# Attention and MoE on one core: q, k and v loads per head, spread over the DMA queue, with new ranks

## Chip, core and metric

The kernel runs on one core of a Trainium2 chip: TensorE (PE) with its weight loads (PEld), VectorE (DVE), ScalarE (ACT), GpSimd (POOL) and the SP queue, which issues nearly all DMAs. The metric is device time in microseconds, the median of several runs. Before the change it is 813.95 us (three runs, 813.47 to 814.06).

## What is computed

```python
q_pool = q.reshape(B, H, S // 2, 2, D).mean(axis=3)          # B 4, H 8, S 1152, D 64
scores = (1 / sqrt(D)) * matmul(q_pool, k.T)                 # 576 x 1152 for each head
attn = softmax(scores)                                       # row maximum, exp, division by the sum
x = matmul(attn, v), heads side by side                      # 2304 tokens x 512
h = x @ w_in                                                 # 512 x 2048
g = h * sigmoid(1.702 * h)
out = g @ w_out                                              # 2048 x 512
```

## The kernel before

Heads are worked in 16 pairs of two. Pairs 0 to 3 are "wide": their products run in fp32, and TensorE turns q, k and the exponentials. Pairs 4 to 15 split every operand into two fp16 halves (`hi` and `lo`), and the DMA engines turn q, k and p by `dma_start_transpose` on the SP queue. Each pair has nine score tiles, numbered n (0 to 143). One tile of pairs 4 to 15 passes through: `scores` S on TensorE; `row_max` M on VectorE, which also frees the PSUM buffer of the scores (there is one); `lift` B, an addition of a constant to the maximum, on VectorE or GpSimd; `exps` E on ScalarE; `p_hi` H, the fp16 cast, on ScalarE or VectorE; `p_lo` L, the subtraction of that cast, on VectorE or GpSimd; `p_tr` T, the transpose of both halves on SP; and, once four tiles of both heads are there (the ninth tile alone), `pv` on TensorE. There are three buffers of p, of hl (the two fp16 halves) and of pt (the transposed).

Before a pair's first score tile comes its preparation: `q_load`, `k_load` and `v_load` from memory (two heads each; q has one DMA of 256 KB and one of 32 KB per head, k and v one of 288 KB), `q_add` on GpSimd, maxima of q, k and v on VectorE (`q_max`, `kv_max`), a scale of all three (`rows_max`, `max_all`, `qkv_scale`), the fp16 halves (`q_hi`, `q_lo`, `k_hi`, `k_lo`, `v_hi`, `v_lo`) and the transposes `q_tr` and `k_tr`. The scale needs all three maxima, so `q_tr` stands behind the last of the three loads. There is one buffer of q and of k as loaded, and two of v.

The MoE weights are loaded in 32 pieces, scaled and split (`w_hi`, `w_lo`) while attention runs. The MoE itself works on nine blocks of 256 tokens, eight steps each: `moe_h` (24 matmuls), `moe_tanh`, `moe_gate`, `moe_hi`, `moe_lo` and `moe_o` (12 matmuls). 24 h and 12 o matmuls are called a unit here; there are 72. Their ranks are above those of all attention work, so TensorE takes them where attention has nothing ready, and the rest stands behind attention.

What stands where on each engine is decided while the program is built. `Plan.order` plays all tasks through with a cost for each and, engine by engine, takes of the tasks that can start soon (within `wait`) the one of lowest rank; the tasks are then written out in that order. Each engine works its instructions strictly in this order. `rank` is the table of ranks and offsets, `movable` lists the tasks that may also run on a second engine. DMAs are played as one line: each takes its `dma` on it and lands `DMA_OUT` later. `gate` holds the loads of a pair back, in that play, until tile n0 - 10 (n0 is the pair's first tile).

Of the kernel before, what the change touches and what calls it, by code (L numbers as in the profile page):

```python
# [23 lines left out]
class Plan:  # L24
# [10 lines left out]
    DMA_IN, DMA_OUT, SWITCH = 0.3, 2.0, 0.095  # L35
# [4 lines left out]
    def add(self, name, eng, cost, rank, fn, after=(), take=(), use=(), dma=0.0, or_on=None, two=False, mode=0):  # L40
        t = dict(name=name, rank=rank, fn=fn, take=list(take), dma=dma, two=two, mode=mode)
# [19 lines left out]
    def order(self):  # L61
# [30 lines left out]
        while len(out) < len(self.tasks):  # L92
# [30 lines left out]
            for h in heirs.get(t["name"], ()):  # L123
                for e in h["on"]:
                    at = free[e] if e == eng and (e == "PE" or h["name"][0] == t["name"][0] == "T") else seen
                    ready[id(h), e] = max(ready[id(h), e], at)
# [9 lines left out]
def kernel(  # L136
# [40 lines left out]
    ACT_LOADS = 99  # L177
# [5 lines left out]
        w1=672.363352, w1_rate=1.175392, w2=1244.868308, w2_rate=0.001398, w1_cut=1489.334692,  # L183
        w1_cut_rate=0.001424, w2_cut=-595.061438, w2_cut_rate=0.001, v_max=2164.84965, load=-651.503117,
        prep=119.711174, max=-168.143312, exp=275.487608, p_hi=-1337.520533, p_lo=698.818424, pv=859.763092,
        x=177.140321, recip=-285.189077, w_tr=458.776726, w_ev=564.091585, g=-2167.171137, pv_b=-936.761133,
        max_b=829.453772, p_lo_b=1852.826129, prep_b=-1240.661907, v=2173.398754, lift=363.803036,
# [52 lines left out]
    def dve(n, psum=False, fast=False):  # L240
        return n / (1920 if fast else 960) + (0.065 if psum else 0.068)
# [152 lines left out]
    def queue(g):  # L394
        return nc.scalar if g.P >= ACT_LOADS else nc.sync

    def k_load(g):
        t = new("kraw", ("kraw", g.P), [128, 2, KR, D], F32)
        for a in range(2):
            (queue(g) if g.P else nc.scalar).dma_start(out=t[:, a], in_=k[g.b, 2 * g.pr + a].rearrange("(p r) d -> p r d", r=KR))  # L400

    def q_load(g):
        t = new("qraw", ("qraw", g.P), [128, NJ, 2, D], F32)
        for a in range(2):
            full, last = q[g.b, 2 * g.pr + a, 0:1024], q[g.b, 2 * g.pr + a, 1024:S]
            queue(g).dma_start(
                out=t[:, 4 * a:4 * a + 4].rearrange("p (u t) r d -> p u (t r d)", u=2),
                in_=full.rearrange("(u p t r) d -> p u (t r d)", u=2, t=2, r=2),
            )
            queue(g).dma_start(  # L410
                out=t[64 * a:64 * (a + 1), NJ - 1].rearrange("p r d -> p (r d)"),
                in_=last.rearrange("(i r) d -> i (r d)", r=2),
            )
# [114 lines left out]
    def v_load(g):  # L528
        t = new("vraw", ("vraw", g.P), [128, 2, KR, D], F32)
        for a in range(2):  # L530
            queue(g).dma_start(out=t[:, a], in_=v[g.b, 2 * g.pr + a].rearrange("(p r) d -> p r d", r=KR))
# [17 lines left out]
    def maxima(g, r):  # L549
        G, f, qa = g.P, first_max(g), ("qkva", g.P)  # L550
        plan.add(("v_max", G), "DVE", dve(1152), r, lambda g=g: kv_max(g, "v"),
                 [("v_load", G)] + ([] if g.wide else [("q_max", G)]), use=[("vraw", G)])
# [5 lines left out]
    for g in pairs:  # L558
# [7 lines left out]
        vr = ("vraw", G)  # L566
        on_act, ahead = G >= ACT_LOADS, n0 + rank["load"]
        le, slow = ("ACT", 0.0) if on_act else ("SP", 0.3)
# [561 lines left out]
```

## Time and profile before

| what | value |
|---|---|
| median of 3 runs | 813.95 us |
| profiled execution: its own time | 812.64 us |
| profiled execution: span | 810.6 us |
| PE busy | 769.4 us, 95% of the span |
| DVE busy | 627.6 us, 77% |
| ACT busy | 538.9 us, 66% |
| POOL busy | 329.2 us, 41% |
| packets of the SP queue (q1) | 127.10 MB, 76.4% of 16 DMA engines' span |

The span runs from the first to the last instruction of the profiled execution; 2.0 us more lie around it. Busy shares are of the whole span. Pairs 0 to 3 take the first 160 us, pairs 4 to 15 the time to about 690 us, and the last 120 us are MoE alone, with ACT and DVE lightly used and the DMA queue nearly empty. So the share of a whole span hides what is full in the middle, and the views below are read by stretch. A busy matmul is not one at full rate, since ends of matmuls are modelled.

### The profile page before, as it was taken

Reading aid. Unit: us, or ns where it says so; the run is one execution under the profiler, and the core shown is the slowest. Engines: PE = TensorE matmul, PEld = TensorE weight load, DVE = VectorE, ACT = ScalarE, POOL = GpSimd, SP = SyncE. Lnnn points to the kernel's source line nnn. Section 1 sums busy time; section 2 is a strip of 40 time slices with the busy share of each in tenths; the row PEclk is TensorE's granted clock in tenths of the full one; section 3 lists DMA queues with packets and bytes.
Section 4 is the critical chain, followed back from the end, with each engine's and each line's share of the span. In section 5 each row is a group of like instructions: output and inputs, shape, how many; then the busy total and the mean of one; then the engine's idle time right before and its main releaser. Section 6 shows DMA issues by size and latency. Waiting matters only on the chain.

```text
span 810.6 us, 16793 instructions
## 1 busy us (share of the span) xinstructions
PE 769.4 (95%) x6756; PEld 514.7 (64%) x6756; DVE 627.6 (77%) x1019; ACT 538.9 (66%) x782; POOL 329.2 (41%) x274
## 2 busy tenths in 40 slices
PE   6999999998999889999999999989898999999997
PEld 3556655656566557666767667756566676666664
DVE  4776998799999998888989789789989885322222
ACT  4888888888686867777667767776677674322222
POOL 3155533366366446454534445363445544000000
PEclk9999999999999999999999999999999999999999
DMA  8255533578999999999999999999999998000001
GB/s 295 74 202 161 163 109 130 160 154 152 210 198 207 174 210 165 184 232 205 205 189 218 213 191 190 218 200 203 174 215 183 173 157 155 2 27 1 27 1 27
DMA packets 336142, 128.77 MB, mean 159 GB/s; under 512 B 311232, under 2 KB 321472, under 8 KB 336064
## 3 DMA queue, kind: packets, MB, share of 16 engines
q1 hardware_dynamic: 335776, 127.10, 76.4%
q8 instruction: 53, 0.87, 0.4%
q10 hardware_dynamic: 288, 0.59, 0.2%
q14 instruction: 25, 0.20, 0.1%
HBM read 45.09 MB, written 4.72 MB: 61 GB/s over the span
## 4 chain that ended last, share of the span: by engine, by line
PE 54%; DVE 24%; DMA 7%; issue 7%; ACT 6%; POOL 1%; SPq 1%; DVEq 0%; ACTq 0%; POOLq 0%
PE h L951 14%; PE o L987 12%; DVE p L668 7%; PE s L654 6%; PE pv L733 5%; PE s L625 5%; DMA pt<-hl 4%; PE o L745 4%; PE pv L768 4%; DVE g L976 2%; ACT hl L248 2%; DVE wbuf L322 2%; DVE gf L965 2%; DVE hl L707 2%; PE h L304 1%
## 5 line engine op out<-in xcount | busy, mean ns | idle before, releaser
L668 DVE TENSOR_SCALAR_CACHE_REDUCE p<-s,e_s 128x1152 f32<-128x1152 f32 x144 | 203.0, 1410 | 26.6 <-PE s L625 10.9
L707 POOL TENSOR_TENSOR hl<-p,hl 128x1152 f16<-128x1152 f32 x77 | 191.9, 2493 | 62.0 <-ACT hl L248 46.1
L675 ACT ACTIVATE p<-p,nm 128x1152 f32<-128x1152 f32 x144 | 179.8, 1249 | 48.7 <-DVE nm L697 31.1
L987 PE MATMUL o<-wbuf,g 128*128 128x512 f16 x864 | 206.2, 380 | 0.0
L951 PEld LDWEIGHTS <-wbuf 128*128 128x128 f16 x1728 | 167.8, 98 | 41.9 <-issue 6.9
L248 ACT ACTIVATE hl<-p 128x1152 f16<-128x1152 f32 x105 | 121.4, 1158 | 26.4 <-DMA pt<-hl 22.5
L654 PE MATMUL s<-kT,qT 128*128 128x384 f16 (+1 forms) x720 | 123.5, 327 | 13.9 <-DVE p L668 12.5
L987 PEld LDWEIGHTS <-g 128*128 128x128 f16 x864 | 82.8, 98 | 84.5 <-issue 3.0
L951 PE MATMUL h<-x16a,wbuf 128*128 128x256 f16 x960 | 116.4, 273 | 3.1 <-DVE gf L965 3.1
L959 ACT ACTIVATE th<-h,t_s 128x512 f32<-128x512 f32 x72 | 49.3, 684 | 95.7 <-PE h L951 94.6
L965 DVE SCALAR_TENSOR_TENSOR gf<-th,h 128x512 f32<-128x512 f32 x72 | 49.2, 683 | 77.2 <-ACT th L959 77.1
L654 PEld LDWEIGHTS <-qT 128*128 128x128 f16 (+1 forms) x720 | 61.9, 100 | 59.8 <-issue 25.3
L951 PE MATMUL h<-wbuf 128*128 128x256 f16 x768 | 92.8, 275 | 0.0
L733 PEld LDWEIGHTS <-vhl 128*64 128x64 f16 x1944 | 80.8, 111 | 15.8 <-issue 14.5
L976 DVE SCALAR_TENSOR_TENSOR g<-gf,g 128x512 f16<-128x512 f32 x72 | 62.9, 873 | 17.0 <-ACT g L248 16.7
L733 PE MATMUL pv<-pt,vhl 128*64 128x256 f16 x1296 | 75.7, 273 | 0.0
L248 ACT ACTIVATE g<-gf 128x512 f16<-128x512 f32 x51 | 32.0, 627 | 37.8 <-DVE gf L965 37.7
L686 POOL TENSOR_SCALAR w_r<-w_d 128x4 f32<-128x4 f32 (+1 forms) x48 | 17.6, 366 | 96.5 <-ACT p L675 94.0
L745 PE MATMUL o<-idf,p 128*128 128x128 f32 x324 | 50.2, 283 | 2.3 <-ACT pt L248 2.3
L248 ACT ACTIVATE pt<-o 128x384 f32<-128x384 f32 x96 | 43.4, 484 | 13.0 <-PE o L745 11.3
L625 PE MATMUL s<-kT,qT 64*128 64x512 f32 (+3 forms) x240 | 49.4, 523 | 1.4 <-DVE p L668 1.3
L299 POOL TENSOR_TENSOR wbuf<-raw 128x512 f32<-128x512 f32 x32 | 34.7, 1091 | 37.8 <-ACT raw L295 37.8
(103 smaller groups left out, 857.9 us busy)
## 6 DMA issues: line engine op xcount, KB each, us to landing
vraw<-in_v_dram SPq DMA_DIRECT2D x32, 288.0 KB, 5.2
kraw<-in_k_dram SPq DMA_DIRECT2D x30, 288.0 KB, 4.5
qraw<-in_q_dram SPq DMA_DIRECT2D x32, 256.0 KB, 3.4
raw<-in_moe_w_in_dram SPq DMA_DIRECT2D x16, 512.0 KB, 5.2
raw<-in_moe_w_out_dram SPq DMA_DIRECT2D x16, 512.0 KB, 4.3
out_dram<-osb SPq DMA_DIRECT2D x16, 256.0 KB, 3.4
pt<-hl SPq DMA_TRANSPOSE x96, 5.0
qraw<-in_q_dram SPq DMA_DIRECT2D x32, 32.0 KB, 3.0
```

The costliest lines, as they stand in the source:

```text
L248: nc.scalar.activation(out=out, in_=in_, func=ACTF.Copy, scale=1.0 if scale is None else scale)
L625: nc.tensor.matmul(out=ps[m, bank, 0:128 * (last - first)], lhsT=qT[h, (j - half) % NJ, m], rhs=kT[h, first:last].rearrange("p j c -> p (j ...
L654: nc.tensor.matmul(out=ps[m, c, 0:384], lhsT=st, rhs=T["kT", g.P][:, o:o + 3].rearrange("p r c -> p (r c)"), start=(l == 0), stop=(l == 1),)
L668: nc.vector.tensor_scalar(out=p, in0=s, scalar1=e_s[:, g.P:g.P + 1], scalar2=None, op0=ALU.mult, op1=ALU.min, accum_out=m)
L675: nc.scalar.activation(out=p, in_=p, func=ACTF.Exp, bias=T["nm", n], scale=-1.0, accum_out=sm)
L707: (nc.vector if e == "DVE" else nc.gpsimd).tensor_tensor(out=t[:, 1, :], in0=T["p", n].rearrange("p c f -> p (c f)"), in1=t[:, 0, :], op=A ...
L733: nc.tensor.matmul(out=ps[64 * a:64 * (a + 1), 0:w], lhsT=T["vhl", g.P][:, a, g.block[a][c], m], rhs=pt[:, l * KR + c, o:o + w], start=(pa ...
L745: nc.tensor.transpose(ps[:, 128 * i:128 * (i + 1)], T["p", n][:, c, 128 * i:128 * (i + 1)], idf)
L951: nc.tensor.matmul(out=h[:, e, :], lhsT=w1(2 * j + e, l, kk), rhs=x_rhs(blk, m, kk), start=(kk == 0 and l == 0 and m == 0), stop=(kk == KD ...
L965: nc.vector.scalar_tensor_tensor(out=gf, in0=T["th", blk, j], scalar=1.0, in1=T["h", blk, j].rearrange("p e n -> p (e n)"), op0=ALU.add, o ...
L976: nc.vector.scalar_tensor_tensor(out=g[:, 1].rearrange("p e n -> p (e n)"), in0=T["gf", blk, j], scalar=2.0 ** -16, in1=g[:, 0].rearrange( ...
L987: nc.tensor.matmul(out=o, lhsT=g[:, l, e, 128 * t:128 * (t + 1)], rhs=w2(fc, m), start=(fc == 0 and l == 0 and m == 0), stop=(fc == KFF - ...
```

## The change

Four things.

The loads. `q_load`, `k_load` and `v_load` now load one head (`a`) each and are six tasks. They may be played from tile n0 - 14 on, one tile apart (q, q, k, k, v, v), so that they come to stand between the transposes. They are the same DMAs as before.

The planner's picture of the DMA queue. A transpose (`tr`) now occupies the SP queue until it is through: at least 2.9 us, and 1.84 us after the DMA before it; it lands 2.05 us later. A load takes 1.05 us per head instead of 2.0 or 2.3 for two; it enters after 0.8 us and lands 1.6 us after its end.

The ranks. All of `rank`, `wait` and `movable` are new. `lift` may no longer run on POOL; `k_hi` and `q_hi` may now run on DVE, `v_hi` may not.

The unused loads from the ACT queue (`ACT_LOADS`) are gone. Nothing is computed in another way.

```diff
-    DMA_IN, DMA_OUT, SWITCH = 0.3, 2.0, 0.095
+    DMA_IN, DMA_OUT, SWITCH = 0.8, 1.6, 0.095
...
-            if t["dma"]:
+            if t["tr"]:
+                free[eng] = dma_free = max(end, dma_free + t["dma"])
+                end = dma_free + 2.05
+            elif t["dma"]:
                 dma_free = max(s + self.DMA_IN, dma_free) + t["dma"]
                 end = dma_free + self.DMA_OUT
...
     rank = dict(
-        w1=672.363352, w1_rate=1.175392, w2=1244.868308, w2_rate=0.001398, w1_cut=1489.334692,
+        w1=1971.8069114113, w1_rate=22.2436521906, w2=2562.6136217615, w2_rate=0.1126475672,
...
-    movable = dict(DVE=('x', 'x_hi', 'w_hi', 'p_hi', 'v_hi', 'moe_hi', 'w_spread', 'qk_ev', 'w_sign'), POOL=('p_lo', 'w_exp', 'lift'))
-    wait = dict(PE=0.021, ACT=0.488, DVE=0.092, POOL=0.65)
+    movable = dict(DVE=('x_hi', 'p_hi', 'x', 'w_hi', 'k_hi', 'moe_hi', 'q_hi', 'qk_ev'), POOL=('p_lo', 'w_exp'))
+    wait = dict(PE=0.005839, ACT=0.318681, DVE=0.098398, POOL=1.168057)
...
-        plan.add(("q_load", G), le, 2.1, ahead, lambda g=g: q_load(g), gate, take=[("qraw", qr)], dma=1.8 + slow)
-        plan.add(("k_load", G), le if G else "ACT", 1.0, ahead + 0.1, lambda g=g: k_load(g), gate, take=[("kraw", kr)],
-                 dma=2.0 + slow)
...
-        plan.add(("v_load", G), le, 1.0, v_at, lambda g=g: v_load(g), v_gate, take=[("vraw", vr)], dma=2.0 + slow)
+        for i, (what, a) in enumerate((w, a) for w in "qkv" for a in range(2)):
+            key = (what + "raw", G)
+            at, after, eng = n0 + rank["load"] + 0.1 * i, [("E", n0 - 14 + i)] if n0 > 14 else [], "SP"
+            if what == "v" and g.wide:
+                at, after = n0 + rank["v"] - 4, [("E", n0 - 5)] if n0 >= 5 else [("k_load", 0, 1)]
+            if what == "k" and not G:
+                eng = "ACT"
+            fn = dict(q=q_load, k=k_load, v=v_load)[what]
+            plan.add(
+                (what + "_load", G, a), eng, 1.06 if what == "q" else 0.5, at, lambda g=g, a=a, fn=fn: fn(g, a),
+                after + ([(what + "_load", G, 0)] if a else []), take=[] if a else [(what + "raw", key)],
+                use=[key] if a else [], dma=1.05,
+            )
...
-                ("T", n), "SP", 3.0, n - 1, lambda n=n: p_tr(n),
+                ("T", n), "SP", 2.9, n - 1, lambda n=n: p_tr(n),
                 [("L", n)] + before, take=take,
-                use=use + [("hl", n)], dma=2.75,
+                use=use + [("hl", n)], dma=1.84, tr=True,
```

On the SP queue, in the stretch that loads pair 10, behind the transposes of pair 9's q and k (qT, kT; pt is p's transposed), the order before is:

```order
L509 DMA_TRANSPOSE qT<-qn_72 128x18x128
L505 DMA_TRANSPOSE kT<-kn 128x18x128
L720 DMA_TRANSPOSE pt<-hl 128x18x128 x4
L406 DMA qraw<-in_q_dram 128x2x256
L410 DMA qraw<-in_q_dram 64x128
L406 DMA qraw<-in_q_dram 128x2x256
L410 DMA qraw<-in_q_dram 64x128
L400 DMA kraw<-in_k_dram 128x576 x2
L531 DMA vraw<-in_v_dram 128x576 x2
L720 DMA_TRANSPOSE pt<-hl 128x18x128 x2
```

And after the change, at the same place:

```order
L508 DMA_TRANSPOSE qT<-qn_72 128x18x128
L504 DMA_TRANSPOSE kT<-kn 128x18x128
L405 DMA qraw<-in_q_dram 128x2x256
L409 DMA qraw<-in_q_dram 64x128
L405 DMA qraw<-in_q_dram 128x2x256
L409 DMA qraw<-in_q_dram 64x128
L720 DMA_TRANSPOSE pt<-hl 128x18x128
L400 DMA kraw<-in_k_dram 128x576
L720 DMA_TRANSPOSE pt<-hl 128x18x128
L400 DMA kraw<-in_k_dram 128x576
L720 DMA_TRANSPOSE pt<-hl 128x18x128
L529 DMA vraw<-in_v_dram 128x576
```

The eight loads that stood in a row behind four more transposes now begin right behind kT with q's four; k, k, v and the second v follow one by one, each behind a transpose of p.

On POOL, in pairs 5 and 6, where p's subtractions (hl, L707) run, the order before is:

```order
L697 TENSOR_SCALAR nm_2347<-nm_2347 128x1
L697 TENSOR_SCALAR nm_2383<-nm_2383 128x1
L707 TENSOR_TENSOR hl_2398<-p_2348,hl_2398 128x1152
L697 TENSOR_SCALAR nm_2429<-nm_2429 128x1
L707 TENSOR_TENSOR hl_2455<-p_2384,hl_2455 128x1152
L707 TENSOR_TENSOR hl_2510<-p_2430,hl_2510 128x1152
```

And after:

```order
L707 TENSOR_TENSOR hl_2363<-p_2253,hl_2363 128x1152
L707 TENSOR_TENSOR hl_2432<-p_2386,hl_2432 128x1152
L824 TENSOR_TENSOR wbuf_69<-xf_2244,wbuf_69 128x256
L707 TENSOR_TENSOR hl_2564<-p_2503,hl_2564 128x1152
L686 TENSOR_SCALAR w_r_87<-w_d_86 128x4
L707 TENSOR_TENSOR hl_2625<-p_2547,hl_2625 128x1152
```

The lifts (nm, L697) have left POOL; all 108 stand on DVE right behind their row maximum.

## Rows read from the trace of the kernel before

**Rows 1.** The page, busy time of the engines over the span

```profile
PE 769.4 (95%) x6756; PEld 514.7 (64%) x6756; DVE 627.6 (77%) x1019; ACT 538.9 (66%) x782; POOL 329.2 (41%) x274
```

**Rows 2.** By stretch: length; busy PE, PEld, DVE, ACT, POOL; clock; DMA share; GB/s

```profile
160.00:690.00 530.00, 503.30 (x4914) 346.04 (x4911) 471.29 (x750) 379.87 (x502) 262.35 (x190) 1.00 1.02 191
160.00:320.00 160.00, 146.62 (x1401) 99.79 (x1398) 152.38 (x230) 120.52 (x163) 87.92 (x68) 1.00 0.97 183
```

**Rows 3.** Timeline of PE at attention's end: start, length, what

```profile
687.59 1.04 PE L733 MATMUL pv<-ptl,vhl 128*64 128x64 f16 x54
688.56 2.79 PE L951 MATMUL h<-wbuf 128*128 128x256 f16 x24
691.19 2.75 PE L987 MATMUL o<-wbuf,g 128*128 128x512 f16 x12
693.78 2.78 PE L951 MATMUL h<-wbuf 128*128 128x256 f16 x24
```

**Rows 4.** Timeline of the SP queue, 354 to 396 us: start, time in issue, what

```profile
354.69 1.01 SPq L1002 DMA_DIRECT2D out_dram<-osb  x2
355.80 6.67 SPq L720 DMA_TRANSPOSE pt<-hl  x2
362.57 3.00 SPq L509 DMA_TRANSPOSE qT<-qn  x1
...
368.47 11.91 SPq L720 DMA_TRANSPOSE pt<-hl  x4
380.44 0.58 SPq L406 DMA_DIRECT2D qraw<-in_q_dram  x1
...
386.10 6.46 SPq L720 DMA_TRANSPOSE pt<-hl  x2
392.65 3.04 SPq L720 DMA_TRANSPOSE ptl<-hl  x1
```

**Rows 5.** Timeline of the SP queue around a single store, 591 us

```profile
591.58 0.54 SPq L1002 DMA_DIRECT2D out_dram<-osb  x1
592.22 5.84 SPq L720 DMA_TRANSPOSE pt<-hl  x2
```

**Rows 6.** Timeline of the SP queue around 311 us

```profile
308.31 2.72 SPq L720 DMA_TRANSPOSE ptl<-hl  x1
313.92 6.30 SPq L720 DMA_TRANSPOSE pt<-hl  x2
```

**Rows 7.** Timeline of POOL there; in brackets the wait before and its releaser

```profile
304.87 0.57 POOL L697 TENSOR_SCALAR nm<-nm 128x1 f32<-128x1 f32 x1 [3.24 <-DVE p L668]
310.87 0.57 POOL L697 TENSOR_SCALAR nm<-nm 128x1 f32<-128x1 f32 x1 [5.43 <-DVE p L668]
311.52 4.86 POOL L707 TENSOR_TENSOR hl<-p,hl 128x1152 f16<-128x1152 f32 x2
```

**Rows 8.** DMA issues, 160 to 690 us: count, KB each, median us to landing

```profile
kraw<-in_k_dram SPq DMA_DIRECT2D x22, 288.0 KB, 4.4
vraw<-in_v_dram SPq DMA_DIRECT2D x22, 288.0 KB, 5.4
qraw<-in_q_dram SPq DMA_DIRECT2D x22, 256.0 KB, 3.2
```

**Rows 9.** Groups, 160 to 690 us: count; busy us, mean ns; idle before, releasers

```profile
L697 POOL TENSOR_SCALAR nm<-nm 128x1 f32<-128x1 f32 x33 | 11.7, 353 | 84.7 <-DVE p L668 79.7 <-DVE w_r L692 4.8
L707 DVE TENSOR_TENSOR hl<-p,hl 128x1152 f16<-128x1152 f32 x31 | 44.6, 1438 | 4.2 <-ACT hl L248 4.0
L322 DVE SCALAR_TENSOR_TENSOR wbuf<-wbuf,s_w 128x1024 f16<-128x1024 f32 x8 | 17.0, 2130 | 0.0
L252 DVE TENSOR_SCALAR g<-gf 128x512 f16<-128x512 f32 x19 | 17.2, 903 | 0.4
```

**Rows 10.** Two lines' instructions: ns shortest/median/longest, first and last start

```profile
L252 DVE TENSOR_SCALAR g<-gf x21: 426/436/2326, 206.1 to 765.8; 128x512 f16<-128x512 f32 x21
L250 DVE CAST hl<-p x3: 745/750/754, 490.0 to 677.6; 128x1152 f16<-128x1152 f32 x3
```

More of the change, by code (lines that the diff above doesn't have):

```diff
@@ L34, with add @@
     WINDOW, BUSY = 3.413, 0.375
-    DMA_IN, DMA_OUT, SWITCH = 0.3, 2.0, 0.095
+    DMA_IN, DMA_OUT, SWITCH = 0.8, 1.6, 0.095
     def __init__(self, sizes, wait):
         self.sizes, self.wait, self.tasks, self.users, self.takers = sizes, wait, [], {}, {}
-    def add(self, name, eng, cost, rank, fn, after=(), take=(), use=(), dma=0.0, or_on=None, two=False, mode=0):
-        t = dict(name=name, rank=rank, fn=fn, take=list(take), dma=dma, two=two, mode=mode)
+    def add(self, name, eng, cost, rank, fn, after=(), take=(), use=(), dma=0.0, or_on=None, two=False, mode=0, tr=False):
+        t = dict(name=name, rank=rank, fn=fn, take=list(take), dma=dma, two=two, mode=mode, tr=tr)
         t["on"], t["free"] = {eng: cost, **(or_on or {})}, or_on is not None
@@ L176 @@
     WIDE = (0,1,2,3)
-    ACT_LOADS = 99
     BLOCKS = ((0, 2, 4, 6, 1, 3, 5, 7, 8), (1, 3, 5, 7, 2, 4, 6, 8, 0))
@@ L392, with k_load, q_load @@
     NT = len(tile_of)
[L394 to L413, printed above, removed]
+    def k_load(g, a):
+        t = T["kraw", g.P] if a else new("kraw", ("kraw", g.P), [128, 2, KR, D], F32)
+        (nc.sync if g.P else nc.scalar).dma_start(out=t[:, a], in_=k[g.b, 2 * g.pr + a].rearrange("(p r) d -> p r d", r=KR))
+    def q_load(g, a):
+        t = T["qraw", g.P] if a else new("qraw", ("qraw", g.P), [128, NJ, 2, D], F32)
+        full, last = q[g.b, 2 * g.pr + a, 0:1024], q[g.b, 2 * g.pr + a, 1024:S]
+        nc.sync.dma_start(
+            out=t[:, 4 * a:4 * a + 4].rearrange("p (u t) r d -> p u (t r d)", u=2),
+            in_=full.rearrange("(u p t r) d -> p u (t r d)", u=2, t=2, r=2),
+        )
+        nc.sync.dma_start(
+            out=t[64 * a:64 * (a + 1), NJ - 1].rearrange("p r d -> p (r d)"),
+            in_=last.rearrange("(i r) d -> i (r d)", r=2),
+        )
     def q_add(g, eng):
@@ L526, in qk_ev, with v_load @@
         copy(e, d, T["qkp", g.P, i][:, 0:128 * (hi - lo)])
[L528 to L531, printed above, removed]
+    def v_load(g, a):
+        t = T["vraw", g.P] if a else new("vraw", ("vraw", g.P), [128, 2, KR, D], F32)
+        nc.sync.dma_start(out=t[:, a], in_=v[g.b, 2 * g.pr + a].rearrange("(p r) d -> p r d", r=KR))
     def v_hi(e, g):
@@ L565 @@
         kt, qt = ("kT", G), ("qT", G)
-        vr = ("vraw", G)
-        on_act, ahead = G >= ACT_LOADS, n0 + rank["load"]
-        le, slow = ("ACT", 0.0) if on_act else ("SP", 0.3)
-        plan.add(("q_load", G), le, 2.1, ahead, lambda g=g: q_load(g), gate, take=[("qraw", qr)], dma=1.8 + slow)
-        plan.add(("k_load", G), le if G else "ACT", 1.0, ahead + 0.1, lambda g=g: k_load(g), gate, take=[("kraw", kr)],
-                 dma=2.0 + slow)
-        if g.wide:
-            v_at, v_gate = n0 + rank["v"] - 4, [("E", n0 - 5)] if n0 >= 5 else [("k_load", 0)]
-        else:
-            v_at, v_gate = ahead + 0.2, gate
-        plan.add(("v_load", G), le, 1.0, v_at, lambda g=g: v_load(g), v_gate, take=[("vraw", vr)], dma=2.0 + slow)
+        for i, (what, a) in enumerate((w, a) for w in "qkv" for a in range(2)):
[10 more added lines that the diff above has]
+                use=[key] if a else [], dma=1.05,
+            )
         plan.add(("q_add", G), pe[0], dve(576) if now else gps(576), r, lambda g=g, e=pe[1]: q_add(g, e),
-                 [("q_load", G)], take=[("qs", qs)], use=[qr], two=True)
+                 [("q_load", G, 1)], take=[("qs", qs)], use=[qr], two=True)
         if g.wide:
@@ L603 @@
             plan.add(("k_lo", G), "DVE", dve(1152) + 0.06, r, lambda g=g: k_lo(g), [("k_hi", G)], use=[kr, kn], two=True)
[L604 to L605 removed]
+            plan.add(("q_tr", G), "SP", 2.9, r, lambda g=g: q_tr(g), [("q_lo", G)], take=[("qT", qt)], use=[qk], dma=1.84, tr=True)
+            plan.add(("k_tr", G), "SP", 2.9, r, lambda g=g: k_tr(g), [("k_lo", G)], take=[("kT", kt)], use=[kn], dma=1.84, tr=True)
         r = n0 + rank["v"]
```

22 lines of the change are left out of this document (11 added, 11 removed).

## Prediction, written before the changed kernel ran

> **What bounds the kernel now.** I read the page's totals first, then busy time by stretch, then the timelines of TensorE, of the DMA queue and of GpSimd around single events.
>
> TensorE is busy 769.4 of 810.6 us [rows 1], and the change alters none of its matmuls: the order has the same number of each line before and after. So the span is TensorE's work plus its idle time, and only the idle time, some 41 us, can be won. From 160 to 690 us, where the twelve fp16 pairs run, TensorE is busy 503.3 of 530 us, VectorE 471.3 and the 16 DMA engines all the time (share 1.02) [rows 2]: three resources are within 11% of full at once. After the last attention product (pv at 687.6 us) TensorE alone runs MoE units of 24 h and 12 o matmuls, one every 5.22 us, 2.63 for h and 2.59 for o, without gaps [rows 3]. What happens in the middle decides.
>
> In the middle the SP queue is what the others feed and wait for. From 354.7 to 395.7 us it issues one DMA after the other with gaps of 0.1 us [rows 4]. Four transposes without loads take 11.9 us, so 2.98 us each.
>
> **The change part by part.**
>
> *MoE work moved behind attention.* The order shows 22 units of h and 23 of o behind the last pv before the change, 25 and 26.25 after. So 3 x 2.63 + 3.25 x 2.59 = 16.3 us of TensorE work [rows 3] leave the attention stage and come after its end. **+16.3 us**, unless the stage ends earlier. With no gain elsewhere the stage keeps its length and its idle time grows by this much.
>
> *Loads spread.* Per pair six large loads (and two of 32 KB) stood in a row; now each stands between transposes. Their number stays: 22 each of q, k and v in the stage [rows 8], 66. Cost of one in a row: from the first issue at 380.44 to the end of the two transposes behind it, 386.10 + 6.46 = 392.56, are 12.1 us; less 2 x 2.98 leaves 6.2 us for six, 1.03 each [rows 4]. Cost of one between transposes, by the nearest rows, stores of 256 KB: two together from 354.69 to 362.47 with two transposes, 7.78 - 5.96 = 1.8, so 0.9 each [rows 4]; a single one from 591.58 to 598.06 with two, 6.48 - 5.96 = 0.5, its own issue and no more [rows 5]. A store is not a load, so the ends are no saving at all (0 us, the loads keep the DMA engines as long wherever they stand) and 0.53 each (35 us). The change makes mostly singles, which is nearest to the last row; but q comes as two issues and in part as a run of four. I take 0.35 each: **-23 us** of queue time. Since the queue has hardly a gap there, what it saves the stage can use; TensorE, with 26.7 us idle in the stage plus the 16.3 moved out, leaves room for 43.
>
> By the Trainium skill (Advanced Engine Details and Errata, X-Bar Transpose (TRN2)) a transposing DMA is as fast as a plain one. No run here isolates that; the sum by it is the third rival.
>
> *Lifts off GpSimd.* 33 of the 108 additions to the row maximum ran on GpSimd and waited there for VectorE; now all run on VectorE right behind the maximum. The rows show what that held up: GpSimd's lift at 304.87 waited 3.24 us and the one at 310.87 waited 5.43 us, both for VectorE; the two subtractions for transposes came only behind it, at 311.52 [rows 7], and the SP queue, done at 311.03, stood still until 313.92 [rows 6]: 2.9 us. How many of the 33 end so the rows do not tell; ends are 0 and about 15 us (five such places), I take two: **-6 us**. On VectorE a lift of one column per partition costs me nothing; VectorE's idle time in the stage, 59 us, hides it.
>
> *Where the p casts and subtractions run.* By the order VectorE takes 24 fp16 casts of p instead of 3 and 23 subtractions instead of 31, and ScalarE takes all casts of v. Casts of 0.75 us [rows 10] make +15.8, eight subtractions of 1.44 us [rows 9] make -11.5; the v and k casts about cancel. VectorE's total does not change by more than some us, ScalarE and GpSimd have room (380 and 262 of 530 us [rows 2]). Cost nothing, hidden by VectorE's 59 idle us in the stage.
>
> *Earlier weight work in pairs 4 and 5.* Before their last row maximum the order puts one more weight residue (2.13 us) and two more subtractions (1.44) on VectorE [rows 9] and three casts (0.75) [rows 10], 7.3 us more; the next two pairs have less. Between 160 and 320 us VectorE is busy 152.4 of 160 [rows 2], so it shows there, from 0 (all given back in pairs 6 and 7) to 7. **+3 us.**
>
> *Less lead for the transposes of q.* The last v load of a pair now stands three to five transposes ahead of that pair's q transpose, before the burst stood four to six ahead. The q transpose waits for maxima of q, k and v and for the scaling; if they are late, SP waits, and the p transposes behind it, and with them pv on TensorE. One transpose less is 2.98 us of lead [rows 4]; it is lost only where the chain is as long as the lead. Between 0 and 10 x 2.98 = 30 us; I take one: **+3 us**, since q's and k's maxima come earlier now and no longer stand with v's in front of the scaling.
>
> **Sum.** 16.3 - 23 - 6 + 3 + 3 = -6.7 us. The profiled execution took 812.64 us (span 810.6 and 2.0 around it); 812.64 - 6.7 = 805.9. The median of the runs is 813.95, 1.3 above the profiled one, so **807 us** for the median of the changed kernel.
>
> **The rivals.**
>
> *First, slower: the engines, not the issue, set the pace.* If a load costs 1.03 us of the DMA engines wherever it stands, spreading saves nothing, but the 16.3 us of MoE work are still gone from the stage, and TensorE idles in their place: 16.3 - 6 + 3 + 3 = +16.3, 830 us; with a saving of 0.15 each, 820. For it: DMA share 1.02 in the stage [rows 2], and two stores together still cost 0.9 each [rows 4]. Against it: the single store at 0.5 [rows 5]. It decides when the saving is under 16.3/66 = 0.25 us per load.
>
> *Second, slower: casts wait for GpSimd.* VectorE's fp16 cast of g takes 0.426 us at least, 0.436 in the median, but up to 2.326 [rows 10]; the mean of those in the stage is 0.903 [rows 9], 0.48 above the minimum, about as if some waited out an instruction on GpSimd. If the 21 new casts of p, and what stands behind them, lose 0.48 each on the path, that is 10 us: -6.7 + 10 = +3.3, 817 us. Against it: the three casts of p now run took 0.745 to 0.754 [rows 10]. The Trainium skill (SBUF — State Buffer, SBUF: two separate sides) calls the port pair of VectorE and GpSimd an exclusive lock held for a whole instruction; the spread of the g casts agrees with it.
>
> *Third, faster than forecast: every load is hidden.* If a transpose keeps the DMA engines only for part of its 2.98 us, a single load costs its issue alone, the 0.53 each of the single store's row: 35 us instead of 23, so 812.64 - 18.7 = 794, 795 for the median. By the skill's rule above a transpose of 576 KB would need what two loads of 288 KB need, 2.1 us by the burst; the 0.9 left in each of eleven transposes would hold the six loads of a pair (an estimate), and this would be the outcome.
>
> *Fourth, no change: TensorE is the bound as it stands.* Its idle share of the stage, 26.7 of 530 us, stays, whoever waits: the stage shrinks with the work that left it, and the tail gets it back. 5% of 16.3 is 0.8 us: 813 us. For it: TensorE's 95% [rows 2].
>
> **How the numbers follow.** Forecast 0.42 (2 to 13 us faster), third rival 0.13, fourth 0.14, first 0.21, second 0.10. This gives faster 0.55, same 0.14, slower 0.31; 0.2% or 1.6 us is about what a measurement of this kernel can tell from no change. The likeliest is 807. The range goes from 795, the third rival's time, up to 824, which takes in the second rival and the half of the first in which part of the saving is there; some 0.1 lies above and some 0.07 below. Forecast alone: 801 to 812.
>
> **What would show it.** Behind the last pv: 25 h units and 26.25 o units, a tail of about 138 us; the last pv should end near 666 us, not 688.6. On the queue: the transpose behind a single load should take 3 to 3.4 us and a load with its share 0.6 to 0.8; near 1.0 the first rival holds, at 0.5 the third. GpSimd's lifts must be gone, and with them stops of the queue like that at 311 us. A queue that stands before the q transposes shows the lead too short. VectorE's casts of p in rows: 0.75 us each if the second rival is wrong, over 1.1 in the mean if it is right. The forecast is wrong if the stage from 160 us to the last pv is not at least 16 us shorter.

## The result, and the profile after

| | before | after |
|---|---|---|
| median of four runs | 813.71 us | 819.29 us |
| ratio | 1 | 1.0076 (1.0055 to 1.0097) |
| profiled execution, span | 810.6 us | 817.1 us |
| last attention product ends | 688.6 us | 678.9 us |
| MoE behind it | 122.0 us | 138.2 us |

The change makes the kernel slower by 0.8% (the ratio is the record's, from all runs; the two medians alone give 1.0069); 807 us was forecast. Of 6.5 us in the span, the tail brings +16.2 and everything ahead of it only -9.7, where the forecast had the last product at 666 us. The first line of the page, and the same stretch by windows (as [rows 1, 2]):

```profile
PE 771.6 (94%) x6756; PEld 515.6 (63%) x6756; DVE 614.7 (75%) x1053; ACT 526.0 (64%) x787; POOL 318.5 (39%) x235
...
160.00:690.00 530.00, 497.21 (x4847) 340.32 (x4840) 454.14 (x771) 359.66 (x493) 257.82 (x161) 0.99 0.99 188
```

VectorE, ScalarE and GpSimd all have less to do, and the DMA engines are as full as before (0.99 against 1.02); still TensorE is the busier by 2.2 us for the same matmuls. The timeline of TensorE at the end of attention (as [rows 3]) shows the tail that the order announced:

```profile
677.85 1.04 PE L733 MATMUL pv<-ptl,vhl 128*64 128x64 f16 x54
678.83 0.82 PE L987 MATMUL o<-wbuf,g 128*128 128x512 f16 x3
679.49 2.78 PE L951 MATMUL h<-x16a,wbuf 128*128 128x256 f16 x24
```

The timeline of the SP queue for the loads of pair 10 (as [rows 4], the same place):

```profile
366.14 0.57 SPq L405 DMA_DIRECT2D qraw<-in_q_dram  x1
366.77 0.48 SPq L409 DMA_DIRECT2D qraw<-in_q_dram  x1
367.29 0.59 SPq L405 DMA_DIRECT2D qraw<-in_q_dram  x1
367.92 0.48 SPq L409 DMA_DIRECT2D qraw<-in_q_dram  x1
368.49 3.28 SPq L720 DMA_TRANSPOSE pt<-hl  x1
371.82 0.58 SPq L400 DMA_DIRECT2D kraw<-in_k_dram  x1
372.52 3.32 SPq L720 DMA_TRANSPOSE pt<-hl  x1
375.88 0.58 SPq L400 DMA_DIRECT2D kraw<-in_k_dram  x1
376.56 3.40 SPq L720 DMA_TRANSPOSE pt<-hl  x1
380.07 0.52 SPq L529 DMA_DIRECT2D vraw<-in_v_dram  x1
380.69 3.28 SPq L720 DMA_TRANSPOSE pt<-hl  x1
384.01 0.57 SPq L529 DMA_DIRECT2D vraw<-in_v_dram  x1
384.68 3.26 SPq L720 DMA_TRANSPOSE pt<-hl  x1
```

From one load of k to the next are 4.06 us, from that to the load of v 4.19. Less a transpose of 2.98 [rows 4] a single load costs 1.1 to 1.2 us, and a load in the row of before cost 1.03. From 294 us on 26 loads of k and v stand alone between two transposes; from the start of such a load to the start of the DMA behind the next transpose are 4.1 us in the median. All loads of pair 10 together, with the five transposes among and behind them, take from 366.14 to 387.94 us; less 5 x 2.98 that is 6.9 us, and the row of before took 6.2. Spreading has saved the queue nothing.

### The profile page after: what moved, and what is told of

It is laid out like the page before. It is cut to its first block, busy times and chain, and to the rows that moved or that the text cites. A ratio compares the mean times of both kernels' runs of the same rounds, so it can differ in the third digit from the quotient of the medians.

```text
span 817.1 us, 16805 instructions
## 1 busy us (share of the span) xinstructions
PE 771.6 (94%) x6756; PEld 515.6 (63%) x6756; DVE 614.7 (75%) x1053; ACT 526.0 (64%) x787; POOL 318.5 (39%) x235
## 4 chain that ended last, share of the span: by engine, by line
PE 62%; DVE 18%; DMA 7%; issue 5%; ACT 4%; SPq 2%; POOL 1%; DVEq 0%; ACTq 0%; POOLq 0%
PE h L951 16%; PE o L987 14%; PE s L654 7%; DMA pt<-hl 6%; DVE p L668 5%; PE s L625 5%; PE pv L733 5%; PE o L745 5%; PE pv L768 5%; DVE kn L497 2%; PE h L308 2%; PE tr L780 2%; DVE hl L254 1%; ACT hl L252 1%; DVE hl L707 1%
## 5 line engine op out<-in xcount | busy, mean ns | idle before, releaser
L707 POOL TENSOR_TENSOR hl<-p,hl 128x1152 f16<-128x1152 f32 x85 | 210.6, 2480 | 186.1 <-ACT hl L252 121.5
L654 PE MATMUL s<-kT,qT 128*128 128x384 f16 (+1 forms) x720 | 125.6, 330 | 15.8 <-DVE p L668 15.8
L252 ACT ACTIVATE hl<-p 128x1152 f16<-128x1152 f32 x84 | 97.1, 1157 | 40.6 <-DMA pt<-hl 29.8
L951 PE MATMUL h<-x16a,wbuf 128*128 128x256 f16 x960 | 118.5, 275 | 4.8 <-DVE gf L965 4.7
L733 PE MATMUL pv<-pt,vhl 128*64 128x256 f16 x1296 | 78.4, 274 | 2.0 <-DMA pt<-hl 2.0
L252 ACT ACTIVATE g<-gf 128x512 f16<-128x512 f32 x55 | 34.4, 626 | 33.3 <-DVE gf L965 33.3
L745 PEld LDWEIGHTS o<-idf,p 128*128 128x128 f32 x324 | 35.9, 141 | 17.9 <-issue 6.2
```

The costliest lines, as they stand in the source:

```text
L252: nc.scalar.activation(out=out, in_=in_, func=ACTF.Copy, scale=1.0 if scale is None else scale)
L654: nc.tensor.matmul(out=ps[m, c, 0:384], lhsT=st, rhs=T["kT", g.P][:, o:o + 3].rearrange("p r c -> p (r c)"), start=(l == 0), stop=(l == 1),)
L707: (nc.vector if e == "DVE" else nc.gpsimd).tensor_tensor(out=t[:, 1, :], in0=T["p", n].rearrange("p c f -> p (c f)"), in1=t[:, 0, :], op=A ...
L733: nc.tensor.matmul(out=ps[64 * a:64 * (a + 1), 0:w], lhsT=T["vhl", g.P][:, a, g.block[a][c], m], rhs=pt[:, l * KR + c, o:o + w], start=(pa ...
L745: nc.tensor.transpose(ps[:, 128 * i:128 * (i + 1)], T["p", n][:, c, 128 * i:128 * (i + 1)], idf)
L951: nc.tensor.matmul(out=h[:, e, :], lhsT=w1(2 * j + e, l, kk), rhs=x_rhs(blk, m, kk), start=(kk == 0 and l == 0 and m == 0), stop=(kk == KD ...
```

## The experiments

Unless a diff says otherwise, an experiment takes the finished order of one of the two kernels and moves only what is named: the list that `plan.order()` gives is rearranged before it is written out (`for t, e in plan.order()` becomes `seq = plan.order()`, the edit shown, and `for t, e in seq`). All other instructions keep their place on every engine. `...` in a diff marks lines left out here. Ratios are to the kernel before, as the record has them for runs taken together, so the quotient of two medians can differ in the third decimal place; the changed kernel has 1.0076. Differences in us are worked out from the ratios, with 813.71 us for the kernel before.

| kernel | median us | ratio (interval) |
|---|---|---|
| e10_before_no_loads | 810.08 | 0.9956 (0.9934 to 0.9979) |
| e6_before_no_v | 809.29 | 0.9941 (0.9919 to 0.9962) |
| e9_after_no_loads | 805.39 | 0.9905 (0.9873 to 0.9937) |
| e3_no_v | 815.33 | 1.0025 (1.0001 to 1.0050) |
| e13_after_loads_unused | 830.09 | 1.0205 (1.0164 to 1.0247) |
| e5_before_spread | 832.47 | 1.0229 (1.0195 to 1.0262) |
| e12_before_lift_v_later | 816.83 | 1.0052 (1.0029 to 1.0076) |
| e1_row | 843.05 | 1.0357 (1.0315 to 1.0398) |
| e15_after_row_late | 854.63 | 1.0507 (1.0453 to 1.0561) |
| e16_after_spread_later | 826.67 | 1.0155 (1.0107 to 1.0202) |
| e4_before_lift | 807.36 | 0.9939 (0.9908 to 0.9970) |
| e14_after_lift_pool | 832.71 | 1.0240 (1.0197 to 1.0283) |
| e8_after_h_act | 827.57 | 1.0168 (1.0139 to 1.0196) |
| e2_moe_back | 825.02 | 1.0146 (1.0094 to 1.0197) |
| e7_before_moe_out | 835.42 | 1.0262 (1.0239 to 1.0286) |
| e11_after_load_cost | 834.48 | 1.0264 (1.0230 to 1.0299) |

### What the loads cost at all

The bound of an edit that places loads better is leaving them out. In both kernels, for each of the three loads (for e6 and e3 only v's); pairs 7 to 15 then use what was loaded for pair 6:

```diff
     def k_load(g):
+        if g.P > 6:
+            T["kraw", g.P] = T["kraw", 6]
+            return
```

> The kernel before without any load of q, k and v for pairs 7 to 15. No way of placing loads can win more than leaving them out. Theory A (the full queue sets the stage): 9 rows of 6.9 us off the queue, so the stage shrinks until TensorE is full there, by its 14 us of idle time in pairs 7 to 15 and more; 797 to 800 us. Theory L (without the v loads it was 5 us faster, 0.28 us per load): 54 x 0.28 = 15 us at most, likely 5 to 10 us, 804 to 809 us.

> The kernel before without the v loads of pairs 7 to 15 (they use the v of pair 6): 18 loads of 288 KB fewer in the same rows. Theory A (the queue sets the stage, a load in a row costs 1.03 us): 18 x 1.03 = 18.5 us faster, about 795 us. Theory L (the queue is not what the stage waits for): 809 to 814 us.

> The changed kernel without any load of q, k and v for pairs 7 to 15 (they use those of pair 6; the rest of the work is the same): by the rows of the changed kernel 18 x 1.55 us for q's heads and 36 x 1.1 us for k's and v's, 67 us of the queue. Theory F (the new order is laid out for loads that cost 0.5 or 1.06 us of the queue and land early; on the chip they and the transposes behind them come late, and VectorE stands for them): VectorE's waits for q, k, transposes and their buffers, some 16 us, go, and at least 10 us of the time, 805 to 809 us. Theory L (the order of TensorE and VectorE binds; the queue is full but not waited for): 813 to 817 us.

> The changed kernel without the v loads of pairs 7 to 15 (they use the v of pair 6; the rest of the work is the same): 18 loads of 288 KB fewer on the DMA queue. Theory A (the queue is the bound from pair 8 on, 1.1 us per load): up to 18 x 1.1 = 20 us shorter, limited by TensorE's idle time there, 20.6 us in pairs 8 to 15; 799 to 805 us. If single loads between transposes are hidden, or TensorE is the bound: 815 to 819 us.

In the kernel before, the 54 loads of pairs 7 to 15 together cost 0.44%, 3.6 us (1.7 to 5.4); v's 18 alone 4.8 (3.1 to 6.6), the same within the intervals. The forecast's 23 us were for 66 loads, so 19 us for these 54. With everything else at its place, no place for them could have won that. In the changed kernel the same loads cost 1.0076 - 0.9905 = 1.7%, 13.9 us (about 11 to 17, both intervals taken together), v's alone 4.1. The difference, about 10 us (7 to 14), is as large as the whole loss of 6.2 or larger: without these loads the new order is the faster one, 805.4 against 810.1 us. Windows from pair 7's first row maximum to the last product, the stretch in which loads are left out (length; busy PE, PEld, DVE, ACT, POOL; clock; DMA share; GB/s). Before, with and without loads:

```profile
299.60:688.60 389.00, 375.68 (x3721) 259.64 (x3719) 336.95 (x552) 272.75 (x357) 185.50 (x130) 1.00 1.04 194
```

```profile
301.90:685.70 383.80, 373.45 (x3720) 258.71 (x3718) 334.21 (x552) 271.43 (x357) 187.69 (x130) 1.00 0.93 162
```

After, with and without:

```profile
294.00:678.90 384.90, 362.21 (x3629) 249.86 (x3626) 324.32 (x559) 257.60 (x347) 190.36 (x120) 0.99 1.03 195
```

```profile
296.00:665.40 369.40, 355.89 (x3623) 247.49 (x3618) 322.61 (x559) 257.54 (x347) 192.39 (x120) 1.00 0.94 167
```

TensorE is idle 13.3 us before and 10.4 without loads; after, 22.7 and 13.5. Loads cost 3.0 us of idle time in the old order and 9.2 in the new one. The new order's stretch also shows 6.3 us more busy time with loads than without, for the same matmuls. Most of that can be the clock in these two executions (below).

### By which way they cost it

A load can hurt in two ways: it lands late for VectorE's maxima, or it holds up the transposes of p behind it. In e13 every load stays in the queue, but from pair 7 on it goes to a spare buffer:

```diff
+    def place(w, g, a, shape):
+        if g.P > 6:
+            T[w, g.P] = T[w, 6]
+            spare = T["spare"] if "spare" in T else new("vraw", "spare", [128, 2, KR, D], F32)
...
+        return T[w, g.P] if a else new(w, (w, g.P), shape, F32)
...
-        t = T["kraw", g.P] if a else new("kraw", ("kraw", g.P), [128, 2, KR, D], F32)
+        t = place("kraw", g, a, [128, 2, KR, D])
```

> The changed kernel with every load at its place and of its size, but from pair 7 on the loads go to a spare buffer that nobody reads, and the pairs use the q, k and v of pair 6. So the queue is as full as in the changed kernel, and nobody waits for a load to land. If what the spread loads cost (13.9 us, the changed kernel against the one without them) is that q and k land late for VectorE (it waits 6.6 us for them): some 7 to 12 us of it come back, 807 to 812 us. If it is that they hold up the transposes of p behind them (ScalarE's casts wait 26 us for transposes, VectorE's 4 us): little comes back, 816 to 820 us.

It is slower than the changed kernel, because the spare buffer, one of v's two, has to come free first: its first use stops the queue from 236.3 to 246.0 us, ahead of the stretch. From pair 7 on the windows compare: 385.6 us, as the changed kernel's 384.9, although no load is waited for:

```profile
303.40:689.00 385.60, 359.94 (x3621) 248.89 (x3618) 326.08 (x560) 257.51 (x347) 190.82 (x120) 1.00 1.03 195
```

So late landing is not the cost: loads that nobody waits for, at the same places of the queue, cost the stretch as much, and what they can hold up is what stands behind them. The view of waits of the same stretch (engine, line, releaser: us, times, longest) shows where that arrives: ScalarE's fp16 cast of p needs a buffer of hl, and the transposes give it back. Kernel before, then without its loads:

```profile
ACT hl L248 <- DMA pt<-hl: 22.2, 20, 3.0
```

```profile
ACT hl L248 <- DMA pt<-hl: 9.7, 9, 2.1
```

The changed kernel, the same without loads, and with loads that nobody reads:

```profile
ACT hl L252 <- DMA pt<-hl: 26.5, 15, 4.5
...
DVE hl L254 <- DMA pt<-hl: 4.2, 4, 1.5
DVE qkv L431 <- DMA kraw<-in_k_dram: 3.2, 3, 1.9
```

```profile
ACT hl L252 <- DMA pt<-hl: 2.7, 3, 1.7
```

```profile
ACT hl L252 <- DMA pt<-hl: 33.5, 20, 4.2
DVE hl L254 <- DMA pt<-hl: 4.7, 5, 1.6
```

From the cast the delay can go on to the subtraction, to the buffer of p, to VectorE's next row maximum and so, through the one buffer of scores, to TensorE. TensorE's wait for row maxima in this stretch, in the changed kernel with loads and without:

```profile
PE s L654 <- DVE p L668: 12.6, 11, 2.4
```

```profile
PE s L663 <- DVE p L677: 9.3, 9, 2.0
```

This path carries 3.3 of the 9.2 us that the loads add to TensorE's idle time. Another 2.0 are attention products that wait for transposes of p themselves (0 without loads), and the rest are mostly short waits for other work of VectorE. How the delay spreads is read from these waits; no run cuts one of the paths.

### Places

The kernel before with its loads spread over four slots ahead (cut to its core; `slot` are the four entries of the queue ahead of the row, and a load is put no earlier than its buffer comes free):

```diff
+            want = [("q_load", 0, 0), ("q_load", 1, 1), ("k_load", 0, 2), ("k_load", 1, 3)]
+            for w, a, s in want:
...
+                seq.insert(max(i, free + 1), (one, "SP"))
+            i = next(i for i, x in enumerate(seq) if x is slot[3])
...
```

> The kernel before with one edit: from pair 7 on, the loads of a pair no longer stand in a row behind four transposes but are spread over the four slots ahead: q, q, k, k one by one, each behind a transpose, and the two v loads at the old place. Every other instruction keeps its place. Theory A (my prediction: the full queue sets the stage, and a spread load saves 0.35 us of it): 9 pairs x 6 x 0.35 = 19 us faster, about 795 us. Theory L (TensorE and VectorE go in lockstep through the one buffer of scores; the queue is full but nobody waits for it): 811 to 815 us.

18.6 us slower: both theories had it wrong. The queue has the same loads and transposes; the transposes close behind kT now come later, and from 300 to 640 us the casts wait for them nearly twice as long as before (22.2 us):

```profile
ACT hl L248 <- DMA pt<-hl: 42.1, 23, 5.1
```

The changed kernel with a row of loads, early (e1) and late (e15), and with its spread loads later (e16, which is e15 with `to = [2, 3, 4, 4, 5, 5]`; `add` is q's sum, `top` are q's and k's maxima):

```diff
...
+            row = [x for x in seq if x[0]["name"][0] in ("q_load", "k_load", "v_load") and x[0]["name"][1] == P]
+            i = seq.index(row[1])
+            seq = [x for x in seq[:i] if x not in row] + row + [x for x in seq[i:] if x not in row]
...
```

```diff
...
+            to = [5, 5, 5, 5, 5, 5]
+            for one, i in zip(row, to):
...
+                    seq.insert(next(y for y, x in enumerate(seq) if x is mark), one)
...
+            seq.insert(max(i + 1, 0), add)
+            i = at("v_max", P)
+            seq[i:i] = top
...
```

> The changed kernel with one edit: from pair 7 on, the eight load DMAs of a pair (six of them large) stand in a row again, at the place of q's second load; every other instruction keeps its place on every engine. Theory A (a load takes about 1.1 us of the DMA engines wherever it stands): no difference beyond 3 us from the changed kernel, 816 to 822 us. Theory B (my prediction's term: spreading saves about 0.35 us per load, and something else ate it): nine pairs with six loads each, 54 x 0.35 = 19 us lost again, about 838 us.

> The changed kernel with all loads of a pair in one row at the place of its last v load, four or five transposes behind kT, about where the kernel before has them; from pair 7 on, with q's sum, q's and k's maxima moved behind them on GpSimd and VectorE. If the place decides (loads close behind kT hold up the transposes that ScalarE's casts wait for, later ones do not): faster than the changed kernel by 5 to 12 us, 807 to 814 us, although the loads stand in a row. If a row costs more than singles in this order (as in e1_row), or the shorter time from q's and k's landing to q's transpose decides: 822 to 845 us.

> The changed kernel with its loads spread, but later: q's heads each behind a transpose, starting one or two transposes behind kT, k's two together and v's two together at the places of the later v loads; maxima moved as in e15_after_row_late. If the place decides: between the changed kernel and e15_after_row_late, 810 to 817 us. If the lead of q and k decides: 822 to 840 us.

All are slower than the changed kernel: by 22.9, 35.1 and 6.4 us by the ratios. In the early row the lump holds up the transposes that the attention products need; in the late one the maxima wait for the loads, and the transposes of the scaling for them. Waits of TensorE and VectorE, first e1 from pair 7 on:

```profile
PE pv L733 <- DMA pt<-hl: 21.5, 6, 6.5
```

and e15 from 300 us on:

```profile
PE tr L443 <- DVE qkv L431: 14.2, 12, 2.1
DVE qkv L422 <- POOL qs L416: 14.9, 6, 4.5
```

The timeline of the SP queue in e1 for the loads of pair 10, the row's first and last loads and what follows:

```profile
374.26 0.57 SPq L405 DMA_DIRECT2D qraw<-in_q_dram  x1
...
380.26 0.80 SPq L529 DMA_DIRECT2D vraw<-in_v_dram  x2
381.17 9.37 SPq L720 DMA_TRANSPOSE pt<-hl  x3
```

From 374.26 to 390.54 less three transposes of 2.98 are 7.3 us for the row; the singles of this pair took 6.9. So e1_row came near theory B in size (843 us against 838), but not for its reason: the row costs the queue 0.4 us more than the singles, far from the 2.5 us by which a pair became slower (22.9 us over nine pairs). The place theory failed for the late row.

In the kernel before, with lifts moved as below, the v loads one transpose later from pair 6 on:

```diff
...
+            one = next(x for x in seq if x[0]["name"] == ("v_load", P))
+            i = seq.index(one)
+            nxt = next(y for y in range(i + 1, len(seq)) if seq[y][1] == "SP" and seq[y][0]["name"][0] == "T")
+            seq.insert(nxt + 1, one)
+            del seq[i]
...
```

> The kernel before with the 33 lifts on VectorE (as in e4_before_lift) and, from pair 6 on, the two v loads of a row one transpose later, so that the row of loads holds up that transpose by 2.2 us less. If the hold-up of p's transposes is what a row costs (ScalarE's casts wait 17 us for transposes there): 1 to 5 us faster than e4_before_lift, 802 to 806 us. If the shorter lead of v for q's transposes is what decides: 808 to 820 us.

0.5% slower than the kernel before, 1.1% slower than without this step (e4). The casts do wait less for transposes, 8.8 us instead of 16.5 in e4 (300 to 640 us), but VectorE's maximum of v now waits for its load, a wait that does not show in e4:

```profile
DVE qkv L432 <- DMA vraw<-in_v_dram: 12.5, 7, 3.4
```

So the lead of v for the scaling is short there too, and 7.7 us less of waiting for transposes did not pay for it.

### Lifts

```diff
...
+            lift_n = next(x for x in seq if x[0]["name"] == ("B", n))
+            if lift_n[1] == "POOL":
+                seq.remove(lift_n)
+                i = next(i for i, x in enumerate(seq) if x[0]["name"] == ("M", n))
+                seq.insert(i + 1, (lift_n[0], "DVE"))
...
```

> The kernel before with one edit: the 33 lifts that run on GpSimd run on VectorE, each right behind its row maximum; everything else keeps its place. My prediction's term: 6 us faster (0 to 15), so about 808 us. Rival: the stops of the queue that a GpSimd lift shows are made good elsewhere, 813 to 815 us.

And the other way round in the changed kernel (`on_pool` holds the 33 tiles):

```diff
...
+        seq = [(t, "POOL" if t["name"][0] == "B" and t["name"][1] in on_pool else e) for t, e in seq]
```

> The changed kernel with the same 33 lifts that the kernel before has on GpSimd moved there again; everything else keeps its place. If the lifts are worth in the new order what they were in the old one (e4_before_lift, 5 to 6 us): 823 to 827 us. If the new order has no use for it: 818 to 821 us.

In the old order the step wins 5.0 us (2.4 to 7.5), as forecast, and makes the fastest kernel here that computes everything, ahead of both. In the new order taking it back costs 13 us, more than the 5 to 6 of the first theory: from pair 7 on ScalarE waits 25.4 us for lifts on GpSimd (3.8 in the kernel before), which there has 85 subtractions instead of 77:

```profile
ACT p L675 <- POOL nm L697: 25.4, 12, 3.7
```

### Casts of p

```diff
+        seq = [(t, "ACT" if t["name"][0] == "H" else e) for t, e in seq]
```

> The changed kernel with one edit: the 24 fp16 casts of p that VectorE takes go back to ScalarE at the same places. If VectorE's late row maxima are what TensorE waits for, and these casts (0.75 us each) make them late: about half of the 24 x 0.75 = 18 us of VectorE time comes back, 809 to 814 us. If ScalarE's chain of exponential and cast is as tight, its casts (1.16 us each) make the transposes late instead: 819 to 830 us.

7.5 us slower than the changed kernel. The casts on VectorE are no loss. Their instructions, by line (count: ns shortest/median/longest, first and last start):

```profile
L254 DVE CAST hl<-p x24: 730/760/2884, 234.1 to 638.8; 128x1152 f16<-128x1152 f32 x24
```

Six are longer than 0.9 us, and in the trace a subtraction of GpSimd runs as each of these six begins. The 22.4 us of busy time make 0.94 us in the mean, between the forecast's 0.75 and the second rival's 1.1.

### MoE units and the picture

The MoE tasks keep their own order and take other places between those of attention (`more` = 36 tasks, three units; e7 has them later, from the kernel before):

```diff
...
+            z = int(first + (y - first) * (end - first) / (end + more - first)) if first <= y < end + more else y
+            at = max([at, moe[z] - z] + [where[x] + 1 for x in seq[i][0]["after"] if x in where])
...
```

> The changed kernel with one edit: from the ninth MoE block's half on (block 4), the MoE tasks take earlier places in the order, so that three more units of h and 2.75 of o stand ahead of the last attention product; attention keeps its order on every engine. Theory A (the DMA queue sets the length of the late stage, TensorE idles beside it): most of the 3 x 2.63 + 2.75 x 2.59 = 15.0 us fits into TensorE's idle time, of which pairs 12 to 15 have 11.6 us; 804 to 811 us. Theory C (TensorE's own order is the bound, idle time goes with the work): the stage grows by what the tail loses, 817 to 821 us.

> The kernel before with one edit: from block 4 on the MoE tasks take later places, so that 2 more units of h and 3 of o stand behind the last attention product, 2 x 2.63 + 3 x 2.59 = 13 us of TensorE work; attention keeps its order. Theory A (the queue sets the stage, so it keeps its length and the moved work is lost): 13 us slower, about 827 us. Theory L (the stage shrinks by the work that leaves it, its idle time stays): 812 to 816 us.

Both are slower, whichever way the units move: 5.7 us and 21.3. In e7 pairs 12 to 15 take longer although 13 us of work left them; TensorE waits 12.2 us for VectorE's row maxima there instead of 3.5. Units at other places than those laid out disturb the rest, so neither run gives the price of moving a unit. The pair e9 and e10 comes nearer, since both stand as they were laid out: without loads, the new order's stretch is 14.4 us shorter. By the count of units in it 3.4 units of h and 3.9 of o less stand there, 19 us. So work that leaves the stage can shorten it; but the two orders differ in lifts and casts too, and the lifts alone were worth 5.0 us in the old order, so what moved units give back by themselves is not shown.

Last, the planner's cost of a load on the queue, at the measured value, and the order laid out anew:

```diff
-                (what + "_load", G, a), eng, 1.06 if what == "q" else 0.5, at, ...
+                (what + "_load", G, a), eng, 1.55 if what == "q" else 1.1, at, ...
```

> The changed kernel with the loads' cost on the queue, in the planner's picture, set to what the changed kernel's trace shows: 1.55 us for a head of q and 1.1 us for one of k or v, instead of 1.06 and 0.5; the ranks are the same and the order is laid out anew (23.5 units of h and 25 of o behind the last attention product). Theory F (the too cheap loads of the picture cost the time): faster than the changed kernel by 5 us or more, 805 to 814 us. Theory L: the ranks were found for the other picture, so any new order of theirs is no better: 819 to 835 us.

1.9% slower than the changed kernel. A truer cost with ranks found for another one gives no better order. It doesn't tell whether the picture's cheap loads made the ranks bad.

## Why the prediction was wrong, point by point

**Loads, -23 us: wrong, in two steps.** The value, 0.35 us saved per load, came from the row of a single store, 0.5 us [rows 5]. The same trace has two more single stores with transposes behind them:

```profile
271.80 0.53 SPq L1002 DMA_DIRECT2D out_dram<-osb  x1
272.64 6.40 SPq L720 DMA_TRANSPOSE pt<-hl  x2
...
438.20 0.53 SPq L1002 DMA_DIRECT2D out_dram<-osb  x1
438.84 9.78 SPq L720 DMA_TRANSPOSE pt<-hl  x3
```

Reckoned in the same way they cost 1.3 and 1.5 us, so the row that was taken is the cheapest of three. A single load between transposes, measured afterwards, costs 1.1, so the end "0" of that range was right, and the first rival's sentence that a load costs the queue the same wherever it stands. The second step was worse: "since the queue has hardly a gap there, what it saves the stage can use". It was argued from a busy share and never from a wait. TensorE's waits in the kernel before, 160 to 688 us, name VectorE first; of the queue's transfers they name one, for 1.3 us:

```profile
PE s L654 <- DVE p L668: 12.5, 17, 2.4
...
PE s L654 <- DMA kT<-kn: 1.3, 1, 1.3
```

Leaving the loads of pairs 7 to 15 out of the old order lowers the DMA share there from 1.04 to 0.93, but wins only 3.6 us; TensorE's idle time falls by 3.0. So the queue was full without setting the stage's length. In the new order the loads cost 13.9 us, so against the old order the term is about +10, not -23.

**MoE moved, +16.3 us: the tail right, the consequence not.** The order's 25 and 26.25 units behind the last product are there, and the tail is 16.2 us longer. That the stage would keep its length without other gains rested on the queue as its pace, which e10 refutes. How much of it the stage gives back is not isolated: without loads it is 14.4 us shorter (e9 against e10), with lifts and casts changed as well.

**Lifts, -6 us: right.** 5.0 us (2.4 to 7.5) in the old order; taking the step back costs 13 us in the new one. [rows 6, 7] show such a place.

**Casts and subtractions, 0: right.** No loss is shown; on ScalarE instead of VectorE the casts cost 7.5 us more.

**Weight work in pairs 4 and 5, +3 us: not seen.** Pairs 4 to 6 take 129.0 us (165.0 to 294.0) against 131.3 (168.3 to 299.6).

**Lead for q_tr, +3 us: not isolated.** That lead is short is shown by e12 and e15 alone.

**Left out: pairs 0 to 3 and the clock.** Pairs 0 to 3 end 3.3 us earlier (165.0 us instead of 168.3), and TensorE's idle time there falls from 11.3 to 8.2 us; the prediction had nothing there. And in the profiled execution the granted clock is at its lower level three times in the stage instead of once. Windows of the changed kernel (the clock is the third number from the end):

```profile
319.90:323.30 3.40, 3.40 (x18) 2.30 (x16) 2.86 (x5) 3.37 (x5) 0.00 (x0) 0.50 1.12 209
401.80:405.20 3.40, 3.40 (x15) 1.93 (x14) 1.99 (x6) 2.51 (x3) 0.33 (x1) 0.51 1.06 202
606.60:610.00 3.40, 3.40 (x31) 1.66 (x25) 3.37 (x8) 1.94 (x3) 1.97 (x1) 0.51 0.91 174
```

Ahead of each, TensorE had stood still for more than 2 us; one of these, from its timeline:

```profile
396.64 1.47 PE L951 MATMUL h<-wbuf 128*128 128x256 f16 x12
400.64 1.04 PE L733 MATMUL pv<-ptl,vhl 128*64 128x64 f16 x54 [2.53 <-DVE xf L810]
```

A granted clock of 0.50 is 1.2 GHz instead of 2.4, so 3.4 us at it cost TensorE 1.7 us at most (an estimate from these lengths). Two such stretches more can make the 2.2 us more of busy time in the whole span. The changed kernel without loads has none in the stretch from pair 7 on, so three make up to 5.1 of the 6.3 us that it is busy less there. But they belong to the single execution: over the four runs of the changed kernel the granted clock is 0.992 (the profiled one), 0.997, 0.996 and 0.995, at 818.89, 818.84, 820.34 and 819.69 us, and in the 60 runs of the kernel before that the experiments brought it is 0.990 to 1.000. The mean is 0.995 for both kernels, so the clock hardly has a part in the 0.8%.

**The account.** In the profiled executions: tail +16.2, pairs 0 to 3 -3.3, pairs 4 to 6 -2.3, pairs 7 to 15 -4.1; together +6.5. In the last part some 19 us of MoE work left, and the loads cost 10.3 us more than before (15.5 against 5.2, by the windows with and without). Together that would be -8.7; the other 4.6 us, with whatever lifts, casts and the clock did there, no run names.

**The rivals.** The first was the one to watch: its test ("near 1.0 the first rival holds") came out its way. Its price, 830 us, was too high by the same mistake as the forecast, the queue as pace. Its decision point, 0.25 us saved per load, decided nothing. The measured 819.3 us lie inside the stated range, and next to the 820 that this rival had for a saving of 0.15 each; that is chance, since no saving was measured and the loss has other terms. The second and third are out: casts are no loss, and loads are not hidden. The fourth, that the stage shrinks with the work that leaves it, points the right way for the MoE units as far as e9 and e10 can tell, but has nothing for the loads. The Trainium skill (SBUF — State Buffer, SBUF: two separate sides) calls the port pair that VectorE shares with GpSimd a lock held for a whole instruction. The trace agrees: the longest cast, 2.884 us against a median of 0.760, begins as a subtraction of GpSimd begins; but only six of the 24 casts met one. By the Trainium skill (Advanced Engine Details and Errata, X-Bar Transpose (TRN2)) a transposing DMA is as fast as a plain one; here a transpose of 576 KB took 2.98 us of the queue and two loads of 288 KB 2.2, so the rule, and the third rival with it, does not hold in this queue. What decided was on no list: the same loads, at the same cost to the queue, hold up transposes, and the new order loses some 10 us more by it.

**Open.** Why the new order bears held-up transposes less well than the old one is not shown. Its places are not plainly bad ones: a row is worse there at both ends, and so are later singles; and in the old order spread places cost 18.6 us (e5).

## What to carry to other kernels

Before an edit is credited with time on a full resource, ask what the bottleneck engine waits for: here TensorE's waits named VectorE, not the full queue, and leaving the loads out altogether (3.6 us) bounds any better placing of them in that order. Where a queue issues both transposes that others wait for and loads that need lead, ask what stands behind a load: in these runs one too early held up transposes (e1, e5), one too late kept the preparation waiting (e12, e15), and a spread row was worse than a row (e5). Take single steps of a large new order that a trace supports (the lifts, 0.9939) rather than the whole.

## What was not expected of the hardware

A single load of 288 KB between two transposing DMAs costs the queue 1.1 us, as in a row, though its own issue is 0.5 to 0.6 us: the transpose behind it takes 3.3 instead of 2.98. And idle stretches of TensorE of 2.1 to 2.5 us were followed by 3.4 us at a granted clock of 0.50 three times in one execution, while others of that length (2.39 us before 570.39 us in the same execution, 2.15 us before 573.35 us in the kernel before) were not.
